# Cross-attention into a squared-ReLU layer on one core: w_out loaded by neighbouring rows, w_in read with a stride, the states loaded otherwise, and new lists

## The chip, the cores and the metric

The kernel runs on 1 core of one Trainium2 chip. The metric is the device time of one execution in microseconds (us). A core has five engines that run side by side, each through its own list of instructions: TensorE (PE; PEld is its weight load), VectorE (DVE), ScalarE (ACT), GpSimd (POOL) and SyncE (SP). Data moves by DMA; the profile calls GpSimd's queue a software queue, SyncE's and ScalarE's hardware queues. In this kernel the loads on GpSimd's queue turn float32 into float16 on the way, the others copy as it is.

## The reference, cut to what matters

For each of 8 batches there are 8 heads, 512 tokens `x` and 32 state slots, 64 values a head. Tokens read the states and states read the tokens, by a softmax each; what comes out (544 rows of 512 values a batch) goes through a two-layer network.

```python
scores = scale * np.matmul(x, state.transpose(0, 1, 3, 2))   # softmax over the 32 slots
xread = np.matmul(a, state)
...
scores2 = scale * np.matmul(state, x.transpose(0, 1, 3, 2))  # softmax over the 512 tokens
sread = np.matmul(a2, x)
...
h = x @ w_in                 # 4352 x 512 by 512 x 2048
r = np.maximum(h, 0.0)
g = s * (r * r) + b
return g @ w_out             # 4352 x 2048 by 2048 x 512
```

Here `x` of the network is `xread` and `sread` side by side over the heads. All inputs and the output are float32.

## The kernel before, in words

**The work.** The read of the tokens is never formed. For each batch b and each of the four chunks c of 512 columns of w_in, TensorE multiplies the states with w_in into `M` (`part_M`, line 718; `att_M`, 834): eight small matmuls, four column groups by two row groups of the array, side by side. Layer 1 (`layer1`, 961) then multiplies `M` with the normalised weights `a4` of the softmax (`att_scores`, 770), four groups of 128 features for a chunk; ScalarE applies ReLU (996), VectorE squares (1002). Layer 2 of batch 0 (`layer2_first`, 1178) is 64 plain matmuls of 512 columns, 16 for each quarter q of w_out. The other batches and the slots (`layer2`, 1235) use a scheme with seven products for eight, whose sums VectorE makes (`pair_sums`, 1073; `weight_sums`, 1108). `bias_sum` (1128) needs all of w_out. The slots' layer 1 comes last (`layer1_slots`, 1012), with w_in as the stationary operand: 64 matmuls of 256 columns.

**Features and rows.** Feature `128 f + p` of chunk c stands on partition p of block f of layer 1's output, so the matmuls of layer 2 need row `128 f + p` of quarter q of w_out on partition p, block f. `wo_load` (484) brings it so: each partition gets four rows that lie 128 rows apart, 2 KB of float32 each.

**Loads.** w_in comes in four chunks (`wi_load`, 472), w_out in four quarters (`wo_load`), each cast to float16 by GpSimd's queue, 512 KB where it lands. The first batch of `x` comes on SyncE's queue in four pieces (`x0_load`, 439) and is cast by ScalarE and VectorE. The states of batch 0 come on ScalarE's queue (409), those of batches 1 and 2 on GpSimd's (561), the others later on SyncE's (522). They are read as 64 values (256 bytes) at a time: each partition holds one slot of one of four heads.

**States' transposes** (`att_st`, 575). VectorE casts the states and writes them twice (602 on); TensorE transposes them through the identity into a float16 view of a PSUM pair (`is_transpose`); VectorE copies them to `stT`. Three sets: batch 0, batches 1 and 2, batches 3 to 7 (this one by DMA).

**Banks.** PSUM holds three pairs of banks (`pair`) and two single banks (`o`). `M` of most (b, c) goes to a pair and is copied out by one engine; those in `APART` (353) go to the two single banks and are copied by halves. Of batch 0, chunks 0 and 1 are copied by halves out of a pair (846).

**Order.** Nothing is scheduled by the compiler. Each piece of work is recorded as a numbered `op` with its cost, and `TURNS` (17) lists, engine by engine, in which order the numbers are issued. `Plan.order` (148) merges the five lists with those costs and with the planner's idea of when loads land, gives out buffers, and puts `fill` matmuls (403, with operands `warm`) into TensorE's list where it expects TensorE to wait in the first 20 us. An engine takes its instructions strictly in this order; a fill matmul is executed whether or not there is a wait. The loads at the start on GpSimd's list are, in order: w_in 0, states of batches 1 and 2, batch 1, w_in 1, w_out 0, w_in 2, w_out 1, w_in 3, w_out 2, w_out 3, batches 2 and 3. TensorE does M and layer 1 of chunk 0 of batch 0, batch 1's transposes between, then chunk 1, then batch 0's layer 2 mixed with layer 1 of chunks 2 and 3 and of batch 1.

Of the kernel before, what the change touches and what calls it, by code (L numbers as in the profile page):

```python
# [11 lines left out]
FP16 = mybir.dt.float16  # L12
# [6 lines left out]
        27 29 25 31 35 33 39 36 40 50 48 80-81 187 84-85 185 53 59 189 92-93 88-89 117 192 118 125-126 121  # L19
        113 122-123 127 119 68 70 114-115 124 116 128 193 120 96 141 129-130 99 237 131-133 225 74 134 142  # L20
        135 145 136 234 137 146 102 147 105 149 148 150-152 161-162 76 108 165-166 240 163 138 111 143
        167-168 164 243 139 222 144 72 62 157 140 158 153 159 56 228 154 160 231 173 155 174 1051 65 330 175
        156 169-171 267 333 258 334 259 268 260-263 269-270 172 176 271 264 272-274 348 351 1056 78 265 345
        354 360 286 277 287-289 694 445 278-281 290-291 282-284 339 357 292 342 293 295-299 454 567 1061
        305-306 300-301 307 302 308 696 576 452 309 315 310 316 311 317 312 318-322 570 572 1066 375-379 448
        689 450 384-387 380 476 388 381-382 467 479 464 389-390 394 482 395 461 391 470 396-397 403 398-401
        473 592 404-405 412 406-407 413-415 408-409 416 410 589 417-419 422 698 692 574 432-436 583 437
        423-424 438 425 439 426-428 586 429 604 601 506 497 507 711 595 498-499 508 598 509 500 510 501-504
        511-512 714 513 516-519 1071 1076 525-526 520-521 527 522-523 528 939 811 529-530 534 531-532
        535-541 544 820 932 935 554-556 545 557-561 546 720 723 619-621 726 622 547-549 705 550-551 623-626  # L30
        717 708 628-630 638-639 631-633 640 634-635 641-642 848 647 643 648-653 644-645 654 845 656-663 1086
        1081 937 941 666-668 676-677 669-670 814 816 818 671-672 678-680 673 954 681 836 741-744 682-683 830
        745-746 957 747 750 748 751-753 833 754-755 760 756 761-763 757 764-766 842 769-770 767 771-775
        778-781 776 782-785 839 788 798-799 789 800 790 801 827 969 963 791 802-805 951 960 1106 792 863 948
        864 793 865 794 866 795 867 1101 868-870 872-878 1091 882 879 883 966 884-888 891-892 1096 889
        893-898 900-906 910 907 911-915 920-921 916-917 1121 1111 984 922 1116 985-986 923 987 924-926
        988-989 927 990 1126 993 991 994-1000 1003-1010 1012-1019 1021-1028 1031-1035 1041 1036 1042
        1037-1038 1043-1048 1143-1150 1152-1159 1162-1169 1171-1178 1180-1187 1190-1197 1200-1207
    """,
    "ACT": """  # L40
        20-21 30 23 37 41 38 42 44 52 45 51 82 86 60 190-191 94 90 194-195 69 197-198 97 100 238 226 235 103
        106 77 109 241 244 223 63 57 229 232 67 331-332 335-336 349 352 79 346 361 355 695 447 446 340 358
# [4 lines left out]
    """,  # L47
    "DVE": """
        24 28 22 26 34 32 6 47 43 49 46 188 83 186 61 7 87 54-55 1057 91 71 95 196 199 98 75 1052 214 101
        239 210 104 215 206 236 107 207 227 110 252 112 218 209 179 177 64 73 245 58 219 242 224 1053 233 66  # L50
        220 230 246 216 253 325 337 183 208 181 247 1058 211 266 248 275 249 347 255 250 256-257 350 356 212
        217 213 285 221 1062 353 254 251 1067 294 341 457 1063 458 303 459 344 369 313 323 1068 363 370 364
        362 359 366 579 371 367 580 365 383 372 581 368 373 392 466 701 402 374 472 1072 484 463 478 469 411
        702 420 481 1077 485 703 475 491 440 585 430 494 594 488 495 492 489 486 588 487 606-608 713 505 597
        514 603 1078 496 493 616 524 940 490 533 1073 542 591 1082 610 936 562 823-824 600 825 944 552 613
        627 1087 617 722 611 945 614 719 636 609 946 728 716 646 615 612 655 707 618 1088 664 1083 942 725
        735 819 710 674 729 684 738 732-733 956 749 730 850 736 739 737 847 758 835 731 768 777 786 734 832
        838 854 740 841 860-861 844 971 959 806 829 855 857 1110 796 851 965 858 852 859 871 962 1105 880
        953 975 856 950 853 972 890 968 1108 899 1103 908 862 976-977 918 1100 981 1098 978 1118 973 1113
        982 928 983 992 979 1125 974 1001 1093 1120 980 1011 1128 1130 1095 1131 1020 1134 1123 1115 1135  # L60
        1029 1137 1140 1136 1138 1132 1141 1039 1049 1151 1160 1133 1142 1170 1139 1179 1188 1198 1208
    """,
    "POOL": """
        8-9 11 16 10 12-15 17-19 329 200 204 202 444 566 180 304 314 276 393 688 810 1060 421 441 182 431
        515 563 324 184 665 178 637 675 1065 1055 759 1070 1080 543 1075 1090 1085 807 685 909 881 919 553
        787 929 797
    """,
    "SP": """
        0-5 327 201 203 328 442 205 443 326 564 338 565 456 1059 687 686 578 460 1064 700 582 1054 704 930
        808-809 931 1079 822 943 1074 826 947 1084 1069 1089 1050 1040 1030 1161 1002 1189 1199 1209  # L70
# [16 lines left out]
class Plan:  # L87
# [60 lines left out]
    def order(self, fill):  # L148
# [3 lines left out]
        dma_free = {"sw": 7.05, "hw": 0.0}  # L152
# [5 lines left out]
        mode, out = "full", []  # L158
# [138 lines left out]
def kernel(  # L297
# [55 lines left out]
    APART = {(1, 0), (1, 1), (2, 0), (2, 1)}  # L353
# [40 lines left out]

    nc.vector.memset(warm, 0.0)
# [13 lines left out]
    nc.scalar.dma_start(stf[0], st_v[:, 0:NG, :])  # L409
    nc.scalar.preload_act_table_set("natural_log_exp_and_others")  # L410

    def T(u):
        return plan.tile(u)
# [7 lines left out]
    def copy(e, dst, src):  # L421
        (nc.scalar.copy if e == "ACT" else nc.vector.tensor_copy)(dst, src)  # L422


    MB, XB = 2.54, plan.XB
# [13 lines left out]
    def x0_load(i):  # L439
        op(  # L440
            {"SP": 0.5},
            lambda e: nc.sync.dma_start(xf_ap(i), x0_v[:, x0_heads(i)]),
            wr=[K(("xf", i))],
            dma=("hw", 0.75),
            lands=(3.6, 4.7, 6.0, 6.5)[i],
        )
# [25 lines left out]
    def wi_load(c):  # L472
        op(
            {"POOL": 0.85},
            lambda e: nc.gpsimd.dma_start(
                out=wi[c],
                in_=moe_w_in.rearrange("(k p) f -> p k f", p=P)[:, :, c * FC : c * FC + FC],
            ),
            rd=[g0],
            wr=[K(("wi", c))],  # L480
            dma=("sw", MB),
        )

    def wo_load(q):
        op(
            {"POOL": 0.75},
            lambda e: nc.gpsimd.dma_start(
                out=wo[q],
                in_=moe_w_out.rearrange("(q f p) n -> q p f n", p=P, q=4)[q],
            ),  # L490
            rd=[g0],
            wr=[K(("wo", q))],
            dma=("sw", MB),
        )
# [49 lines left out]
    for i in range(4):  # L544
# [14 lines left out]
    op(  # L559
        {"POOL": 0.9},  # L560
        lambda e: nc.gpsimd.dma_start(out=stf[1], in_=st_v[:, NG : NS * NG, :]),
        rd=[g0],
        wr=[K(("stf", 1))],
        dma=("sw", 0.45),
    )
# [9 lines left out]
    def att_st(i):  # L575
# [4 lines left out]
        def view():  # L580
            return T(u).rearrange("p a f -> p (a f)").bitcast(FP16).rearrange("p (n q) -> p n q", q=P)
# [4 lines left out]
        def tr(e):  # L586
            for k in range(n):
                mm(
                    view()[:, k, :],
                    st16[:, b0 * NG + k].rearrange("p k d -> p (k d)"),  # L590
                    ident16,
                    is_transpose=True,
                )
# [11 lines left out]
            since=(5.0, 0.0, 0.0)[i],  # L605
        )
        if i == 2:
# [14 lines left out]
            {"DVE": 0.1 + 0.07 * n},  # L622
            lambda e: copy(e, stT[:, b0 * NG : b1 * NG], view()[:, 0:n]),
# [210 lines left out]
    def att_M(b, c, engs=("ACT", "DVE")):  # L834
# [11 lines left out]
        if b == 0 and c < 2:  # L846
            for g in range(NG):
# [3 lines left out]
                    rd=[K(u)],  # L851
# [494 lines left out]
    att_scores(0)  # L1346
    att_st(1)
# [71 lines left out]
```

## Time and profile before

| | |
|---|---|
| median of 3 runs | 207.4 us (207.22 to 208.0) |
| the profiled execution: time | 208.01 us |
| its span, first to last instruction | 206.2 us |
| bytes moved | 25.83 MB, mean 125 GB/s |
| median issue to landing: w_in, w_out, `x` | 13.2, 17.4, 8.6 us |

The profile is of one execution. A row of its timeline has the start in us, the length, the engine, the line, the operation with output and inputs, the count, and in brackets how long the engine was idle before it and what ended that. Matmuls are pipelined: a row's length contains the way through the array, so the pace of a series is read from starts, not from lengths. All of TensorE's matmuls have line 335, that of a helper, and all plain copies line 422; they are told apart by the tiles' names.

### The profile page before, as it was taken

To read this page: it belongs to the slowest core of one execution; us is meant where nothing else is said; L and a number is where in the kernel's file an instruction comes from. 1 tells how busy PE (TensorE), PEld (TensorE's weight loads), DVE (VectorE), ACT (ScalarE), POOL (GpSimd) and SP (SyncE) were. 2 spreads that over 40 slices of the span, in tenths; PEclk is the share of its full clock that TensorE was granted. 3 is DMA by queue.
4 is the path that set the end of the run, shared out by engine and by line. 5 is a ranking of instruction groups with operands and counts; after the bars stand their busy time and mean duration, and the time that the engine had idled before them with its cause. 6 is when DMAs were issued, how large, how long until landed. Compare 5 with 4: busy or idle time off the path is not lost.

```text
span 206.2 us, 4768 instructions
## 1 busy us (share of the span) xinstructions
PE 199.3 (97%) x1989; PEld 134.7 (65%) x1989; DVE 164.3 (80%) x325; ACT 109.3 (53%) x153; POOL 38.8 (19%) x60
## 2 busy tenths in 40 slices
PE   7979999999999999999999999999999999999992
PEld 3744444435666665677577767766776688888881
DVE  2327637989899979899999988997969689859871
ACT  4757786467588879468644473254606634130000
POOL 4832002001020120331301030033070200331000
PEclk9999999999999999999999999999999999999999
DMA  5999999992999992798991470233020200253054
GB/s 173 201 197 204 206 205 179 179 198 16 186 139 195 143 221 41 110 134 154 199 194 60 80 222 13 51 111 118 0 103 3 102 0 2 71 187 105 0 176 131
DMA packets 47285, 25.83 MB, mean 125 GB/s; under 512 B 31616, under 2 KB 45440, under 8 KB 47264
## 3 DMA queue, kind: packets, MB, share of 16 engines
q0 software_dynamic: 13792, 15.34, 38.0%
q1 hardware_dynamic: 33056, 10.10, 26.4%
q8 instruction: 15, 0.25, 0.5%
q10 hardware_dynamic: 416, 0.10, 0.2%
q14 instruction: 6, 0.05, 0.1%
HBM read 17.33 MB, written 8.91 MB: 127 GB/s over the span
## 4 chain that ended last, share of the span: by engine, by line
PE 89%; DMA 7%; DVE 1%; issue 0%; ACT 0%; POOL 0%; DVEq 0%
PE o L335 48%; PE pair L335 41%; DMA wi<-in_moe_w_in_dram 4%; DMA out_dram<-osb 2%; DMA ident<-ident_const 1%; DVE osb L1281 0%; DVE M L422 0%; ACT M L422 0%; DVE osb L1270 0%; DVE aN L906 0%; DVE sr L933 0%; POOL gate L552 0%; DVEq L1270 0%
## 5 line engine op out<-in xcount | busy, mean ns | idle before, releaser
L996 ACT ACTIVATE g<-pair 128x1024 f16<-128x1024 f32 x64 | 63.0, 1023 | 44.5 <-PE pair L335 44.4
L335 PE MATMUL pair<-a,M 128*128 128x512 f16 x256 | 63.3, 379 | 0.1
L335 PEld LDWEIGHTS <-pd 128*128 128x128 f16 x480 | 46.4, 98 | 10.1 <-issue 1.5
L335 PEld LDWEIGHTS <-g 128*128 128x128 f16 x424 | 40.7, 98 | 17.5 <-issue 2.9
L1002 DVE TENSOR_TENSOR g<-g 128x1024 f16<-128x1024 f16 x64 | 42.8, 683 | 2.8 <-ACT g L996 2.8
L335 PE MATMUL o<-u,pd 128*128 128x256 f16 x360 | 44.2, 273 | 0.0
L335 PE MATMUL o<-wo,g 128*128 128x256 f16 (+1 forms) x272 | 42.6, 285 | 0.0
L335 PEld LDWEIGHTS <-M 128*128 128x128 f16 x256 | 24.7, 98 | 22.9 <-DVE M L422 0.6
L1173 POOL DMA_DIRECT2D out_dram<-osb x28 | 18.8, 724 | 103.2 <-DVE osb L1281 54.5
L1270 DVE SCALAR_TENSOR_TENSOR osb<-o,s,bias_bc 128x512 f32<-128x512 f32 (+1 forms) x32 | 22.9, 715 | 7.3 <-PE o L335 5.7
L422 ACT CAST M<-pair 128x1024 f16<-128x1024 f32 (+1 forms) x22 | 20.4, 958 | 7.8 <-PE pair L335 7.8
L1281 DVE SCALAR_TENSOR_TENSOR osb<-o,s,osb 128x512 f32<-128x512 f32 (+1 forms) x24 | 17.2, 716 | 7.6 <-PE o L335 7.4
L1082 DVE TENSOR_TENSOR pd<-g 128x1024 f16<-128x1024 f16 (+1 forms) x32 | 20.7, 651 | 0.1
L335 PE MATMUL o<-wo,pd 128*128 128x256 f16 x120 | 19.0, 273 | 0.0
L335 PE MATMUL o<-u,g 128*128 128x256 f16 x120 | 17.5, 273 | 0.0
L422 DVE CAST M<-pair 128x1024 f16<-128x1024 f32 (+1 forms) x8 | 9.2, 1153 | 4.9 <-PE pair L335 3.8
L1093 DVE TENSOR_TENSOR pd<-g,pd 128x512 f16<-128x512 f16 (+1 forms) x32 | 12.5, 400 | 0.1
L1043 ACT ACTIVATE g<-pair 128x256 f16<-128x256 f32 x16 | 5.3, 385 | 13.0 <-PE pair L335 13.0
L1090 DVE TENSOR_TENSOR pd<-g,pd 128x512 f16<-128x512 f16 (+1 forms) x32 | 12.1, 400 | 0.1
L782 ACT ACTIVATE E<-pair 128x512 f16<-128x512 f32 x16 | 9.5, 600 | 4.7 <-issue 2.3
L335 PE MATMUL pair<-wi,stT 64*32 64x512 f16 x224 | 9.8, 383 | 1.5 <-DMA wi<-in_moe_w_in_dram 1.2
L463 POOL DMA_DIRECT2D xn<-in_x_dram x7 | 6.3, 909 | 25.2 <-ACT g L996 15.1
(70 smaller groups left out, 143.7 us busy)
## 6 DMA issues: line engine op xcount, KB each, us to landing
out_dram<-osb POOLq DMA_DIRECT2D x28, 256.0 KB, 3.2
xn<-in_x_dram POOLq DMA_DIRECT2D x7, 512.0 KB, 8.6
wi<-in_moe_w_in_dram POOLq DMA_DIRECT2D x4, 512.0 KB, 13.2
wo<-in_moe_w_out_dram POOLq DMA_DIRECT2D x4, 512.0 KB, 17.4
u<-in_x_dram SPq DMA_DIRECT2D x4, 256.0 KB, 3.9
out_dram<-osb SPq DMA_DIRECT2D x4, 256.0 KB, 2.7
out_dram<-osb SPq DMA_DIRECT2D x4, 128.0 KB, 2.3
pd<-in_state_dram SPq DMA_DIRECT2D x1, 320.0 KB, 4.0
```

What stands on the lines that cost most here:

```text
L335: return nc.tensor.matmul(out, lhsT, rhs, start=start, stop=stop, tile_position=tp, is_transpose=is_transpose, skip_group_check=True,)
L422: (nc.scalar.copy if e == "ACT" else nc.vector.tensor_copy)(dst, src)
L463: lambda e: nc.gpsimd.dma_start(out=T(xn[b]).rearrange("p h c d -> p h (c d)"), in_=x[b].rearrange("h (q c) d -> q h (c d)", q=P),),
L782: nc.scalar.activation(T(E[b])[:, g, :].rearrange("p (m t) -> p m t", m=2), T(u)[:, :, hS * g : hS * g + hS], AF.Exp, scale=scale, accum_o ...
L996: lambda e, u=u, part=part: nc.scalar.activation(part(), T(u), AF.Relu),
L1002: lambda e, part=part: nc.vector.tensor_mul(part(), part(), part()),
L1082: nc.vector.tensor_tensor(view()[:, :, 0:2], blocks(b, j)[:, :, 1:2, :].to_broadcast((P, 2, 2, n)), blocks(b, j)[:, :, 0:4:3, :], ALU.subt ...
L1090: nc.vector.tensor_tensor(view()[:, :, 2], blocks(b, j)[:, :, 3], view()[:, :, 0], ALU.subtract)
L1093: nc.vector.tensor_tensor(view()[:, :, 3], blocks(b, j)[:, :, 2], view()[:, :, 2], ALU.subtract)
L1173: lambda e: eng(e).dma_start(dst, src()),
L1270: lambda e: nc.vector.scalar_tensor_tensor(t_view(u), o_view(bank), s_bc, bias(h), ALU.mult, ALU.add),
L1281: lambda e: nc.vector.scalar_tensor_tensor(t_view(u), o_view(bank), s_bc, t_view(u), ALU.mult, ALU.add),
```

## The change

w_out: a partition p now gets rows 4p to 4p + 3 of the quarter, 8 KB of float32 in one run. Feature `4p + f` of a chunk must then stand on partition p of block f, so `part_M` and `layer1_slots` read w_in's columns with a stride of four. The states of batches 0 to 2 are loaded as neighbouring rows too (two rows, 512 bytes, a partition for batch 0; four rows, 1 KB, for batches 1 and 2), and the transposes, now plain matmuls into float32, write every second or every fourth column so that the slots come out in the old order. The states of batches 1 and 2 leave GpSimd's queue; SyncE loads them after VectorE has written two elements of their buffer from batch 0's `E`. Chunks 1 to 3 of batch 0 join `APART`. The planner's costs change in places, and `TURNS` is new for all engines. Ops behind the states' load have new numbers.

GpSimd's order at the start is now w_in 0, 2, 3, 1, w_out 0, batch 1, w_out 1, w_out 2, w_out 3, batches 2 and 3. TensorE does M and layer 1 of all four chunks of batch 0 (chunks 0, 2, 3, 1), then w_out 0's matmuls, with the transposes of the states and of batch 1 among them, then w_out 1, batch 1's scores, w_out 2, w_out 3, and then layer 1 of batch 1. There are 57 fill matmuls in place of 59.

The diff without the lists and with the numbering lines left out:

```diff
@@ -149,7 +150,7 @@
         free = {"PE": 2.88, "ACT": 2.4, "DVE": 1.3, "POOL": 0.5, "SP": 0.6}
         queue = {e: self.turns(e)[::-1] for e in free}
         assert sum(map(len, queue.values())) == len(self.ops)
-        dma_free = {"sw": 7.05, "hw": 0.0}
+        dma_free = {"sw": 6.95, "hw": 0.0}
         big, flying, weights = 0.0, [], []
         landed = {"sw": [], "hw": []}
         slot_free = {t: [0.0] * len(s) for t, s in self.slots.items()}
@@ -350,7 +351,7 @@
     NM = 10
     NS = 3
     TURN = 3
-    APART = {(1, 0), (1, 1), (2, 0), (2, 1)}
+    APART = {(0, 1), (0, 2), (0, 3), (1, 0), (1, 1), (2, 0), (2, 1)}
     plan = Plan()
     plan.buffers("ps", ps)
     plan.buffers("o", ob)
@@ -392,6 +393,10 @@
     ident_dr = nc.inline_tensor(np.eye(P, dtype=np.float16), name="ident_const")
     st_v = state.rearrange("b (g hf) j d -> (hf j) (b g) d", g=NG)
 
+    def st_near(b0, b1):
+        rows = state[b0:b1].rearrange("b h j d -> (b h j) d")
+        return rows.rearrange("(q r) d -> q r d", q=P)
+
     nc.vector.memset(warm, 0.0)
     nc.vector.memset(few, 0.0)
     nc.vector.memset(ones16, 1.0)
@@ -406,7 +411,7 @@
     for _ in range(4):
         mm(ob[1], warm[:, 0:P], warm)
     nc.scalar.dma_start(ident16, ident_dr.ap())
-    nc.scalar.dma_start(stf[0], st_v[:, 0:NG, :])
+    nc.scalar.dma_start(stf[0], st_near(0, 1))
     nc.scalar.preload_act_table_set("natural_log_exp_and_others")
 
     def T(u):
@@ -422,7 +427,7 @@
         (nc.scalar.copy if e == "ACT" else nc.vector.tensor_copy)(dst, src)
 
 
-    MB, XB = 2.54, plan.XB
+    MB, WB, XB = 2.54, 1.95, plan.XB
 
     xf_u = [plan.unit(("u", i), "u") for i in range(2)]
     x0_v = x[0].rearrange("h (q c) d -> q h (c d)", q=P)
@@ -442,7 +447,7 @@
             lambda e: nc.sync.dma_start(xf_ap(i), x0_v[:, x0_heads(i)]),
             wr=[K(("xf", i))],
             dma=("hw", 0.75),
-            lands=(3.6, 4.7, 6.0, 6.5)[i],
+            lands=(3.75, 4.7, 5.95, 6.25)[i],
         )
 
     def x0_cast(i):
@@ -478,7 +483,7 @@
             ),
             rd=[g0],
             wr=[K(("wi", c))],
-            dma=("sw", MB),
+            dma=("sw", MB + 0.44 * (c == 3)),
         )
 
     def wo_load(q):
@@ -486,11 +491,11 @@
             {"POOL": 0.75},
             lambda e: nc.gpsimd.dma_start(
                 out=wo[q],
-                in_=moe_w_out.rearrange("(q f p) n -> q p f n", p=P, q=4)[q],
+                in_=moe_w_out.rearrange("(q p f) n -> q p f n", p=P, q=4)[q],
             ),
             rd=[g0],
             wr=[K(("wo", q))],
-            dma=("sw", MB),
+            dma=("sw", WB),
         )
 
     stf2 = plan.unit(("stf2",), "pd")
@@ -556,13 +561,6 @@
     g0 = K(("start",))
     wi_load(0)
     wi_load(1)
-    op(
-        {"POOL": 0.9},
-        lambda e: nc.gpsimd.dma_start(out=stf[1], in_=st_v[:, NG : NS * NG, :]),
-        rd=[g0],
-        wr=[K(("stf", 1))],
-        dma=("sw", 0.45),
-    )
     wo_load(0)
     wi_load(2)
     wo_load(1)
@@ -578,7 +576,7 @@
         n = (b1 - b0) * NG
 
         def view():
-            return T(u).rearrange("p a f -> p (a f)").bitcast(FP16).rearrange("p (n q) -> p n q", q=P)
+            return T(u)[:, 0, 0 : n * P]
 
         def src():
             return st_rows(n) if i == 2 else stf[i]
@@ -586,10 +584,9 @@
         def tr(e):
             for k in range(n):
                 mm(
-                    view()[:, k, :],
+                    view().rearrange("p (q r) -> p r q", r=n)[:, k],
                     st16[:, b0 * NG + k].rearrange("p k d -> p (k d)"),
                     ident16,
-                    is_transpose=True,
                 )
 
         key = K(("st", i))
@@ -602,7 +599,7 @@
             ),
             rd=[[], [K(("stf", 1))], [K(stf2)]][i],
             wr=[key],
-            since=(5.0, 0.0, 0.0)[i],
+            since=(4.1, 0.0, 0.0)[i],
         )
         if i == 2:
             part = slice(b0 * NG, b1 * NG)
@@ -619,8 +616,8 @@
         u = plan.unit(("stps", i), "ps")
         op({"PE": 0.056 * n}, tr, rd=[key], wr=[K(u)], mode="full", mms=n)
         op(
-            {"DVE": 0.1 + 0.07 * n},
-            lambda e: copy(e, stT[:, b0 * NG : b1 * NG], view()[:, 0:n]),
+            {"DVE": 0.07 + 0.135 * n},
+            lambda e: copy(e, stT[:, b0 * NG : b1 * NG].rearrange("p n q -> p (n q)"), view()),
             rd=[K(u)],
             wr=[K(("stT", i))],
         )
@@ -721,7 +718,7 @@
                 mm(
                     M_bank(b, c, g)[32 * q : 32 * q + 32],
                     st_T(b, g, q, g),
-                    wi[c][64 * g : 64 * g + 64, q],
+                    wi[c][64 * g : 64 * g + 64, q].rearrange("k (p f) -> k f p", f=4),
                     tp=(64 * g, 32 * q),
                 )
 
@@ -843,12 +840,12 @@
                     wr=[K(M[b, c], g)],
                 )
             return
-        if b == 0 and c < 2:
+        if b == 0:
             for g in range(NG):
                 op(
                     {"ACT": 0.48, "DVE": 0.64},
                     lambda e, g=g: copy(e, T(M[b, c])[:, g], T(u)[:, g]),
-                    rd=[K(u)],
+                    rd=[K(u)] + [K(M[b, c], 0)] * g,
                     wr=[K(M[b, c], g)],
                 )
             return
@@ -1020,7 +1017,7 @@
                     for k in range(NKM):
                         mm(
                             T(u)[:, 0, 256 * i : 256 * i + 256],
-                            wi[c][:, k, o : o + P],
+                            wi[c][:, k].rearrange("k (p f) -> k f p", f=4)[:, o // P],
                             srd[:, k].rearrange("p j b -> p (j b)"),
                             start=(k == 0 and i == 0),
                             stop=(k == NKM - 1),
@@ -1344,6 +1341,19 @@
     att_st(0)
     att_xT_pe(0)
     att_scores(0)
+    op(
+        {"DVE": 0.08},
+        lambda e: nc.vector.tensor_copy(stf[1][:, 0, 0:2], T(E[0])[:, 1, 0:2]),
+        rd=[K(E[0], 1)],
+        wr=[K(("stf", 1))],
+    )
+    op(
+        {"SP": 0.5},
+        lambda e: nc.sync.dma_start(out=stf[1], in_=st_near(1, NS)),
+        wr=[K(("stf", 1))],
+        dma=("hw", 0.4),
+        lands=16.6,
+    )
     att_st(1)
     for c in range(4):
         for b in range(3):
```

More of the change, by code (lines that the diff above doesn't have):

```diff
@@ L18 @@
     "PE": """
[L19 to L38, printed above, removed]
+        24 28 26 30 32 34-35 38 51 39 83 87 69 88 84 99 76 102 108 60 105 91-92 95-96 116-117 120 124 118
@@ new lines @@
+        121 125-126 49 119 127 190 128 188 122-123 129 136 132 137 192 72 138 130 133 139 134 131 196 195
+        152-155 135 148 140 149-150 144 79 111 168 151 164-165 246 169 166-167 114 145 141 170 240 171 237
+        142 54 146 243 63 225 143 147 228 156-157 57 74 160-162 234 231 163 176-177 158 333 66 1054 159
+        178-179 270-271 336-337 261 172 262 173 272-274 174 275 263-266 276 267 175 268 348 351 277 345 1059
+        342 289 354 280-281 290 282 291-292 448 81 699 283-284 293 285-286 294 287 295 357 298 457 697 296
@@ new lines @@
+        299-301 360 302 363 303-305 308 573 579 570 309 318 310-314 319 315 320 1064 451 453 321-325 378-379
+        692 455 575 380-383 387 470 388-389 464 479 390 384 391 467 473 385 392 695 1069 393 476 397-398 482
+        399-401 394 402 485 406-408 403 409-410 404 411 592 412-413 415-422 425 595 426 577 701 435 427
+        436-437 428 438-439 598 440 586 429 441-442 604 607 430 500-501 431-432 502-503 589 504-507 509-511
+        714 601 717 512-513 519 514-516 520-524 528 525-526 529-535 537 814 1074 1079 538-541 547 542-544
@@ new lines @@
+        942 935 938 548 557-558 549 559-564 711 550-551 723 552-553 622 729 554 720 726 631-632 623 633
+        624-625 634 626-629 823 944 819 635-637 641-642 638 708 643-646 650-652 647 653 648 654 848 655 851
+        656 659-660 657 661-666 669-670 1084 1089 821 940 817 679-682 671 683 836 684-685 672-676 830 686
+        839 753-754 744-745 755 746-748 960 749-751 833 756-759 763 760 764-765 842 766-767 772 768-769 773
+        770 774-775 845 776 781-782 777-779 783-788 791 957 801-804 954 792 805 793-794 969 795 806 796
@@ L39 @@
+        807-808 797 1104 798 1094 866-871 875 872-873 963 876-877 885 878-880 886 881 966 887 882 951 972
+        894 888-890 895-896 891 897-898 892 899-900 1099 903 901 904-910 913 1109 914 923-924 915 925-928
+        1119 916-917 929 918 930 1114 1129 919-920 987-990 1124 991 996-997 992-994 998-1003 1006-1013
+        1015-1022 1024-1030 1034 1031 1035-1041 1044-1051 1146-1153 1155-1162 1165-1172 1174-1181 1183-1190
+        1193-1200 1203-1210
     """,
     "ACT": """
-        20-21 30 23 37 41 38 42 44 52 45 51 82 86 60 190-191 94 90 194-195 69 197-198 97 100 238 226 235 103
@@ L42 @@
-        106 77 109 241 244 223 63 57 229 232 67 331-332 335-336 349 352 79 346 361 355 695 447 446 340 358
[4 rows of a table removed]
+        22 21 27 31 36-37 40-41 52 43-44 53 70 85 89 78 100 103 61 109 106 97 93 193-194 200 197-198 201 80
+        112 247 241 238 55 244 226 64 229 75 59 235 232 334-335 68 338-339 349 352 346 343 355 449-450 700
+        82 358 458 698 361 364 572 580 571 452 454 456 576 694 693 471 465 480 468 474 477 486 483 696 593
+        578 702 596 599 587 605 590 608 602 715 718 815-816 936-937 943 712 939 724 730 727 721 945 709 824
@@ L47 @@
+        820 852 849 941 818 822 831 840 834 837 843 846 961 958 955 1097 1107 1105 1095 970 964 952 1102 967
+        973 1110 1122 1112 1100 1120 1127 1130 1125 1132 1115 1117
     """,
     "DVE": """
-        24 28 22 26 34 32 6 47 43 49 46 188 83 186 61 7 87 54-55 1057 91 71 95 196 199 98 75 1052 214 101
-        239 210 104 215 206 236 107 207 227 110 252 112 218 209 179 177 64 73 245 58 219 242 224 1053 233 66
-        220 230 246 216 253 325 337 183 208 181 247 1058 211 266 248 275 249 347 255 250 256-257 350 356 212
@@ L52 @@
[L52 to L61, printed above, removed]
+        20 23 19 25 29 33 46 42 45 71 86 77 62 48 104 101 90 98 50 94 191 189 110 6 73 107 202 199 113 213
@@ new lines @@
+        221 7 1055 115 180 182 248 56 242 239 65 328 222 219 223 58 255 227 230 217 214 236 216 67 233 1060
+        209 245 186 249 1056 211 340 210 250 184 256 269 252-253 218 278 251 257 1061 220 258 224 215 259
+        1065 353 212 356 260 288 344 254 347 359 297 460-461 306 462 574 372 1066 316 350 369 373 326 370
+        365 362 582 366-367 583-584 466 1070 386 375-376 1071 368 472 475 469 395 704 405 488 414 478 1080
+        484 371 423 481 705 377 706 374 594 487 443 489-490 600 497 491 498 433 1075 494 492 591 597 495 508
@@ L62 @@
+        613 609 517 496 719 527 499 614 493 716 536 606 1081 1076 545 588 735 619 610 565 1085 603 826-827
[4 rows of a table added]
+        1103 995 1126 1101 986 1004 1133-1134 1014 1128 1116 1111 1121 1135 1023 1131 1136 1143 1118 983
+        1032 1144 1137-1138 1140 1139 1042 1052 1154 1141 1163 1173 1142 1145 1182 1191 1201 1211
     """,
     "POOL": """
-        8-9 11 16 10 12-15 17-19 329 200 204 202 444 566 180 304 314 276 393 688 810 1060 421 441 182 431
-        515 563 324 184 665 178 637 675 1065 1055 759 1070 1080 543 1075 1090 1085 807 685 909 881 919 553
@@ L66 @@
-        787 929 797
+        8-9 12 14 10-11 15 13 16-18 332 207 203 205 183 447 569 307 1068 317 279 1058 187 185 396 327 691
+        813 1063 434 444 566 640 181 668 424 1088 1078 688 556 546 1083 1073 1093 810 762 884 518 912 922
+        790 800 932 678
     """,
     "SP": """
-        0-5 327 201 203 328 442 205 443 326 564 338 565 456 1059 687 686 578 460 1064 700 582 1054 704 930
-        808-809 931 1079 822 943 1074 826 947 1084 1069 1089 1050 1040 1030 1161 1002 1189 1199 1209
+        0-5 47 208 204 331 330 206 329 446 1057 445 341 568 459 567 690 689 463 581 1067 1062 703 585 707
@@ L71 @@
+        811 933 812 934 825 1082 946 829 1077 1072 1087 950 1092 1005 1043 1053 1164 1033 1192 1202 1212
     """,
```

8 rows, old and new, of the table TURNS are left out of this document.

## The prediction

> **What bounds the kernel now.** I read the page first: the share of each engine and the chain that ended last.
>
> ```profile
> span 206.2 us, 4768 instructions
> PE 199.3 (97%) x1989; PEld 134.7 (65%) x1989; DVE 164.3 (80%) x325; ACT 109.3 (53%) x153; POOL 38.8 (19%) x60
> ...
> PEclk9999999999999999999999999999999999999999
> ...
> PE 89%; DMA 7%; DVE 1%; issue 0%; ACT 0%; POOL 0%; DVEq 0%
> PE o L335 48%; PE pair L335 41%; DMA wi<-in_moe_w_in_dram 4%; DMA out_dram<-osb 2%; DMA ident<-ident_const 1%; DVE osb L1281 0%; DVE M L422 0%; ACT M L422 0%; DVE osb L1270 0%; DVE aN L906 0%; DVE sr L933 0%; POOL gate L552 0%; DVEq L1270 0%
> ```
>
> TensorE is busy all the time at full clock, and the only transfer of weight on the chain is the first w_in chunk (4% of 206.2 is 8.3 us). So the change can earn time only where TensorE is busy with nothing. The table of busy time by stretches says where that is not:
>
> ```profile
> 20.00:48.00 28.00, 28.00 (x195) 11.47 (x197) 20.25 (x36) 19.48 (x23) 1.13 (x3) 1.00 1.14 183
> 48.00:90.00 42.00, 41.73 (x531) 27.05 (x532) 38.09 (x74) 32.60 (x47) 8.02 (x10) 1.00 0.87 134
> 90.00:140.00 50.00, 50.00 (x589) 35.33 (x588) 47.01 (x81) 26.69 (x34) 7.13 (x11) 1.00 0.60 127
> 140.00:202.20 62.20, 62.17 (x516) 50.30 (x514) 50.55 (x109) 18.49 (x30) 12.46 (x19) 1.00 0.22 72
> ```
>
> From 20 us on TensorE (first figure after the stretch) loses 0.3 us in 182. What is left is the opening. The timeline there, TensorE's own lines, shows real work and fill (`warm` operands):
>
> ```profile
> 11.72 0.41 PE L335 MATMUL pair<-wi,stT 64*32 64x512 f16 x8 [1.21 <-DMA wi<-in_moe_w_in_dram]
> ...
> 12.06 0.94 PE L335 MATMUL o<-warm 128*128 128x256 f16 x7
> ...
> 13.06 0.82 PE L335 MATMUL o<-warm 128*128 128x256 f16 x6
> ...
> 17.08 0.50 PE L335 MATMUL pair<-warm 128*128 128x256 f16 x3
> ...
> 18.07 0.72 PE L335 MATMUL pair<-warm 128*128 128x256 f16 x5
> ...
> 19.36 0.55 PEld L335 LDWEIGHTS <-M 128*128 128x128 f16 x4 [0.61 <-DVE M L422]
> ```
>
> The first chunk lands at 11.7 us; from there to 19.4 us there are 21 fill matmuls and short waits; from 19.4 us there is no gap. The question is how much real work stands done at the end of this opening, before and after.
>
> **The change part by part.** (1) *When data lands.* The tile view of the weights gives issue and time to landing.
>
> ```profile
> L475 POOL DMA_DIRECT2D wi<-in_moe_w_in_dram x4: 770/838/908, 3.4 to 9.0; - x4
> ...
> DMA to landing us min/median/max: 8.3/13.2/18.6
> ```
> ```profile
> L487 POOL DMA_DIRECT2D wo<-in_moe_w_out_dram x4: 760/768/861, 6.8 to 12.8; - x4
> ...
> DMA to landing us min/median/max: 13.2/17.4/19.8
> ```
> ```profile
> 14.88 0.45 PEld L335 LDWEIGHTS <-xn 128*128 128x128 f16 x8 [0.52 <-DMA xn<-in_x_dram]
> ```
>
> So w_in 0 lands at 3.4 + 8.3 = 11.7, w_out 0 at 6.8 + 13.2 = 20.0, w_out 3 at 12.8 + 19.8 = 32.6: five steps of 2.52 us. Batch 1 came 3.15 us behind w_in 0, with the states ahead of it. The changed GpSimd order is w_in 0, 2, 3, 1, w_out 0, batch 1, w_out 1, 2, 3. I keep w_in 0 at 11.7 (nothing ahead of it in its queue changes) and take the steps: w_in 2 at 14.2, 3 at 17.1 (0.4 for the states, which now cross from SyncE's queue; bounds 0 and 3.15 - 2.52 = 0.6), 1 at 19.7. What w_out costs with 8 KB runs no row shows; bounds 2.52 (today's) and 1.3 (half, for want of a row). I keep 2.5, since all loads of the trace run at one pace.
>
> (2) *The opening, walked.* Durations of ScalarE's steps, and the pace of TensorE:
>
> ```profile
> 9.17 0.59 ACT L782 ACTIVATE E<-pair 128x512 f16<-128x512 f32 x1
> ...
> 9.64 0.20 ACT L782 ACTIVATION_READ_ACCUMULATOR E<-pair 128x1 f32 x1
> ...
> 10.44 0.58 ACT L817 ACTIVATE o<-o 128x512 f32<-128x512 f32 x1
> ...
> 12.19 0.59 ACT L422 CAST M<-pair 128x512 f16<-128x512 f32 x1 [1.18 <-PE pair L335]
> ...
> 12.68 0.60 ACT L823 ACTIVATE a<-o 128x512 f16<-128x512 f32 x1
> ...
> 14.89 1.02 ACT L996 ACTIVATE g<-pair 128x1024 f16<-128x1024 f32 x1 [1.13 <-PE pair L335]
> ```
> ```profile
> 38.25 0.86 PE pair L335 x4
> ```
>
> A 512-wide matmul takes 0.86 / 4 = 0.216. In the new lists TensorE does M of chunk 0 at 11.7, the denominator's second half behind it, then layer 1 of chunks 0, 2 and 3 as they land. ScalarE has in a row from 12.2: M half, Ln, Exp, M half (14.6), M of chunk 2 (15.2), two ReLUs that wait for layer 1 (15.85 to 17.9), M of chunk 3 (18.5), two ReLUs (20.5), M of chunk 1 (21.1). TensorE reaches M of chunk 1 at 19.85, runs half of chunk 3's layer 1 to 21.1, waits 0.2 for that last M copy and 0.15 for a PSUM pair whose ReLU ends at 22.1, and ends layer 1 of batch 0 at 23.1. By then it has done 32 matmuls of layer 1 (6.9), four M groups (0.86) and a denominator (0.22): 8.0 us of work. Before, at 23.05 (row 22.83 below), it had done 16 of layer 1 (3.45), ten of layer 2 (2.16), batch 1's transposes (0.9), three M groups, scores, states' transpose and a denominator (1.3): 7.8 us. **Gain 0.1** (0.2 of work less 0.07 of time). Bounds: +0.8 if neither the states nor ScalarE hold it back (0.1 + 0.4 + 0.35), -0.6 if each of its three ReLU pairs meets a busy ScalarE by another 0.2.
>
> (3) *Behind the opening.* TensorE now meets w_out 0 at 23.1 (lands 22.2), batch 1 at 25.5 (24.9), w_out 1 at 27.3 (27.4), w_out 2 at 30.0 (29.9), w_out 3 at 32.5 (32.4). So faster w_out loads have cover already at today's pace: **worth 0** (bounds 0 and 0.2). Batch 1's scores now stand only some 1.8 us of matmuls ahead of the denominator that needs both their Exps (0.5 + 2 x 0.6 + 0.2 = 1.9): **loss 0.1** (0 to 0.4).
>
> (4) *Mode changes of the array* (whole to quarters and back). Two M groups in the trace:
>
> ```profile
> 22.83 0.38 PE L335 MATMUL o<-wo,g 128*128 128x512 f16 x1
> ...
> 23.14 0.63 PE L335 MATMUL pair<-wi,stT 64*32 64x512 f16 x16
> ...
> 23.70 0.60 PE L335 MATMUL o<-wo,g 128*128 128x512 f16 x2
> ```
>
> Entering costs 23.14 - (22.83 + 0.22) = 0.09, leaving 0.56 - 2 x 0.22 = 0.12. Counted over both lists, the number of changes behind the opening is the same (42). **0.**
>
> (5) *The stall that is left.*
>
> ```profile
> 75.81 0.41 PE L335 MATMUL pair<-wi,stT 64*32 64x512 f16 x8 [0.27 <-DVE sr L933]
> ```
>
> A bank is freed late by one VectorE step. The lists are new, so it goes or moves: **gain 0.1** (0 to 0.27).
>
> (6) *w_in read with a stride of four.* As the moving operand in all 32 M groups, as the weight in 64 loads of the last layer 1:
>
> ```profile
> L335 PEld LDWEIGHTS <-wi x64: 97/98/98, 161.5 to 184.9; 128*128 128x128 f16 x64
> L335 PE MATMUL pair<-srd,wi x64: 272/273/273, 161.7 to 185.0; 128*128 128x256 f16 x64
> ```
>
> No strided read of either kind is in the trace. Below: 0, as nothing can be read faster than packed. Above: twice, 32 x 0.22 = 7.0 us for the M groups, and 64 x (0.196 - 0.109) = 5.6 us for the loads, which would then outlast their matmuls (0.109, half of 0.216). I take **0**, the packed row. [...]
>
> (7) *States' transposes* now write every second or fourth fp32 column of PSUM instead of packed fp16.
>
> ```profile
> 5.95 0.28 PE L335 MATMUL pair<-ident,st 128*128 128x128 f16 x2
> ...
> 12.84 0.39 PE L335 MATMUL pair<-ident,st 128*128 128x128 f16 x4
> ...
> 13.26 0.42 DVE L422 COPY stT<-pair 128x512 f16<-128x512 f16 x1 [0.41 <-PE pair L335]
> ```
>
> Only the four of batches 1 and 2 are in gapless time, at some 0.06 each: **0**, at most 0.2 if the writes double. [...] The copy behind them reads fp32 and costs up to 0.69 instead of 0.42 on VectorE, with over 1 us until the scores need it.
>
> (8) One GpSimd load of states (0.76) goes; a SyncE load and a tiny VectorE copy come. SyncE's next work is a transpose of batch 1's scores, much later: 0.
>
> Sum: -0.1 + 0.1 - 0.1 = **-0.1**. The profiled execution took 208.01 us around its span of 206.2; the three runs shown have a median of 207.4. From the median: **207.3 us**.
>
> **The rivals.** *Faster:* ScalarE and the states never hold TensorE back, and the stall at 75.8 goes: 0.8 + 0.27, so 206.3. For it: copies of M now have banks of their own on both engines. Against: the walk finds ScalarE without a gap from 18 to 21 us. *Slower, w_in's stride:* one mechanism, TensorE's reads at 8-byte steps. It decides once eight M matmuls take over 0.25 us (32 x 0.03 = 1 us); at twice it is 207.3 + 7.0 + 5.6 = 219.9. For it: nothing in the trace is read like this. Against: four fp16 apart is close. *Slower, the lists slip:* the opening's bound of 0.6, the scores' 0.4, PSUM's 0.2 and no gain at 75.8: 208.7. For it: ScalarE's order is rigid, and SyncE's states cross the weights. *w_out no faster than now:* the change doesn't do what it may look like; by (3) still 207.3 to 207.5.
>
> **How the numbers follow.** Forecast 0.43, w_out no faster 0.05, faster 0.27, lists slip 0.15, stride 0.10. 0.5% (1.04 us) is about what a measurement of this kernel tells from no change. Faster 0.27, within 0.48, slower 0.25. The range goes from the faster rival, less the 0.2 by which a run lies under the median, to the slipped lists: 206.1 to 208.7; it leaves out the stride and little else. The forecast's own range is 206.7 to 207.9.
>
> **What would show it.** M groups of eight at 0.22 apart and weight loads of `wi` at 98 ns (6); w_in 1 landing near 19.7 (1); the first `wo` matmul near 23 with about 17 or more fill matmuls behind 11.7 (2); no TensorE wait on a `wo` load (3); TensorE gapless from there to 202. Wrong would be: w_in 0 landing a microsecond earlier or later than 11.7, a gap over 0.3 us behind 25 us, or M groups that stretch.

## The result, and the profile after

The changed kernel takes 215.13 us (median of 4 runs, 214.62 to 215.87) against 207.31 us beside it: 1.0382 times as long, with a 95% interval of 1.0329 to 1.0435. It is slower by 7.8 us, far outside the range on record.

The page of the changed kernel, the span, the engines' shares, the clock and the chain:

```profile
span 213.7 us, 4755 instructions
...
PE 206.8 (97%) x1987; PEld 135.6 (63%) x1987; DVE 161.1 (75%) x322; ACT 113.5 (53%) x159; POOL 36.8 (17%) x59
...
PEclk9999999999999999999999999999999999999999
...
PE 94%; DMA 3%; SPq 1%; DVE 1%; issue 0%; ACT 0%
```

TensorE is as full as before (97%), at full clock, and is now 94% of the chain. Its busy time grew by 206.8 - 199.3 = 7.5 us, the span by 7.5 us. TensorE's idle time is 6.9 us in both profiles (206.2 - 199.3 and 213.7 - 206.8), so it isn't waiting that was added: the work takes longer. The tile view of w_in says which work. Before:

```profile
L335 PE MATMUL pair<-wi,stT x224: 372/386/388, 11.7 to 137.7; 64*32 64x512 f16 x112
```

After:

```profile
L336 PE MATMUL pair<-wi,stT x200: 605/621/665, 11.7 to 143.9; 64*32 64x512 f16 x100
L336 PEld LDWEIGHTS <-wi x64: 112/113/117, 168.1 to 191.8; 128*128 128x128 f16 x64
L336 PE MATMUL pair<-srd,wi x64: 272/273/273, 168.2 to 191.9; 128*128 128x256 f16 x64
L336 PE MATMUL o<-wi,stT x56: 605/606/608, 14.4 to 50.1; 64*32 64x512 f16 x56
```

The matmuls of the M groups, which stream w_in with the stride, went from a median of 386 ns to 606 and more. The 64 weight loads went from 98 to 113 ns, and the matmuls that they feed stayed at 273. TensorE's own lines of the opening, in the changed kernel:

```profile
8.99 0.62 PE L336 MATMUL pair<-ident,xn 128*128 128x128 f16 x8 [1.10 <-ACT xn L427]
...
11.75 0.63 PE L336 MATMUL pair<-wi,stT 64*32 64x512 f16 x8
12.31 0.39 PE L336 MATMUL o<-E,bones 128*128 128x512 f16 x1
12.54 0.82 PE L336 MATMUL pair<-warm 128*128 128x256 f16 x6
...
14.37 0.63 PE L336 MATMUL o<-wi,stT 64*32 64x512 f16 x8
14.93 1.90 PE L336 MATMUL pair<-a,M 128*128 128x512 f16 x8
16.67 0.82 PE L336 MATMUL o<-warm 128*128 128x256 f16 x6
17.41 0.63 PE L336 MATMUL o<-wi,stT 64*32 64x512 f16 x8
...
20.15 0.63 PE L336 MATMUL o<-wi,stT 64*32 64x512 f16 x8
...
23.32 0.81 PE L336 MATMUL o<-wo,g 128*128 128x512 f16 x3
```

A group of eight holds the array 12.31 - 11.75 = 0.56 us; before it was 12.06 - 11.72 = 0.34. That is 0.22 more, the time of a whole stream of 512 columns, and 32 groups make 7.0 us, which lies within the 6.8 to 9.0 us that the interval of the ratio allows. The first matmul with w_out starts at 23.3, close to the 23.1 of the walk, but by chance; the account of step (2) below says why.

### The profile page after: what moved, and what is told of

Read it like the earlier page. It is cut to its first block, busy times and chain, and to the rows that moved or that the text cites. A ratio compares the mean times of both kernels' runs of the same rounds, so it can differ in the third digit from the quotient of the medians.

```text
span 213.7 us, 4755 instructions
## 1 busy us (share of the span) xinstructions
PE 206.8 (97%) x1987; PEld 135.6 (63%) x1987; DVE 161.1 (75%) x322; ACT 113.5 (53%) x159; POOL 36.8 (17%) x59
## 4 chain that ended last, share of the span: by engine, by line
PE 94%; DMA 3%; SPq 1%; DVE 1%; issue 0%; ACT 0%
PE o L336 50%; PE pair L336 43%; DMA u<-in_x_dram 3%; SPq L447 1%; DVE osb L1210 0%; ACT xn L427 0%; DVE osb L1267 0%
## 5 line engine op out<-in xcount | busy, mean ns | idle before, releaser
L993 ACT ACTIVATE g<-pair 128x1024 f16<-128x1024 f32 x64 | 63.7, 1026 | 36.1 <-PE pair L336 35.7
L336 PE MATMUL o<-wo,g 128*128 128x256 f16 (+1 forms) x272 | 41.2, 285 | 0.0
L1170 POOL DMA_DIRECT2D out_dram<-osb x28 | 19.3, 760 | 107.0 <-DVE osb L1278 67.2
L427 ACT CAST M<-pair 128x1024 f16<-128x1024 f32 (+1 forms) x24 | 22.6, 980 | 10.0 <-PE pair L336 9.9
L336 PE MATMUL pair<-wi,stT 64*32 64x512 f16 x200 | 14.2, 619 | 0.0
L1087 DVE TENSOR_TENSOR pd<-g,pd 128x512 f16<-128x512 f16 (+1 forms) x32 | 12.8, 403 | 0.1
L1090 DVE TENSOR_TENSOR pd<-g,pd 128x512 f16<-128x512 f16 (+1 forms) x32 | 12.7, 405 | 0.0
L336 PE MATMUL pair<-wo,g 128*128 128x512 f16 x32 | 10.4, 380 | 0.6 <-DVE osb L1210 0.6
L336 PE MATMUL o<-warm 128*128 128x256 f16 (+1 forms) x55 | 9.7, 327 | 1.2 <-DVE few L401 1.2
```

The lines of the kernel that those rows point to most:

```text
L336: return nc.tensor.matmul(out, lhsT, rhs, start=start, stop=stop, tile_position=tp, is_transpose=is_transpose, skip_group_check=True,)
L993: lambda e, u=u, part=part: nc.scalar.activation(part(), T(u), AF.Relu),
L1087: nc.vector.tensor_tensor(view()[:, :, 2], blocks(b, j)[:, :, 3], view()[:, :, 0], ALU.subtract)
L1090: nc.vector.tensor_tensor(view()[:, :, 3], blocks(b, j)[:, :, 2], view()[:, :, 2], ALU.subtract)
L1170: lambda e: eng(e).dma_start(dst, src()),
```

## The experiments

Two theories stood at the start. **A**: TensorE takes a strided moving operand in at half speed; that alone is the loss. **B**: the new lists, the new order of loads or the states' loads cost the time. A third, **C**, blamed the strided weight loads. Runs with several executions have a ratio to the kernel before, with its interval; the others ran once.

**The stride alone, in the old kernel.**

```diff
-                    wi[c][64 * g : 64 * g + 64, q],
+                    wi[c][64 * g : 64 * g + 64, q].rearrange("k (p f) -> k f p", f=4),
```

> The kernel before with one edit: the M groups read w_in with a stride of four as the moving operand; features come out permuted against w_out, so the output is not the reference's. Theory A (a strided moving operand is taken in at half speed): each of the 32 groups of eight matmuls takes 0.22 us longer, 207.3 + 7.1 = 214.4 us, and a matmul of such a group shows 0.6 instead of 0.38 us. Rival B (the new lists and the new order of loads cost the time): 207.3. Rival C (the strided weight loads of the slots' layer 1 cost it): 207.3.

Measured: 214.35 us, ratio 1.0324 (1.0279 to 1.0369), that is 6.7 us by the ratio. The same tile view of this kernel:

```profile
L335 PE MATMUL pair<-wi,stT x224: 605/607/628, 10.3 to 142.7; 64*32 64x512 f16 x112
L335 PEld LDWEIGHTS <-wi x64: 97/98/98, 166.7 to 190.1; 128*128 128x128 f16 x64
```

Old lists, old loads, packed weight loads, and the M matmuls at 607 ns: nearly all of the loss (5.8 to 7.7 of the 7.8 us) is there without anything else of the change. B and C cannot explain it.

**The change without the stride.**

```diff
-                    wi[c][64 * g : 64 * g + 64, q].rearrange("k (p f) -> k f p", f=4),
+                    wi[c][64 * g : 64 * g + 64, q],
...
-                            wi[c][:, k].rearrange("k (p f) -> k f p", f=4)[:, o // P],
+                            wi[c][:, k, o : o + P],
...
-                in_=moe_w_out.rearrange("(q p f) n -> q p f n", p=P, q=4)[q],
+                in_=moe_w_out.rearrange("(q f p) n -> q p f n", p=P, q=4)[q],
```

> The changed kernel with w_out loaded as before and w_in read packed again; lists, order of loads and the states' loads stay. Theory A: 215.1 - 7.1 = 208.0 us. Rival B: about 215. What is left above or below 207.3 is the price of lists, loads and states together: my forecast's own sum said -0.1.

Measured: 208.11 us, ratio 1.001 (0.9982 to 1.0038). Lists, order of loads and states together are worth nothing that can be measured. Theory B is out from this side too. TensorE comes to w_out earlier here (21.9 us, not 23.3) and waits for it once:

```profile
26.68 0.59 PE L336 MATMUL o<-wo,g 128*128 128x512 f16 x2 [0.30 <-DMA wo<-in_moe_w_out_dram]
```

**The change with the stride moved to where weights are loaded.** Feature `4p + f` is picked when layer 1 loads M, and w_in streams packed:

```diff
-                    wi[c][64 * g : 64 * g + 64, q].rearrange("k (p f) -> k f p", f=4),
+                    wi[c][64 * g : 64 * g + 64, q],
...
-                                T(M[b, j])[:, g, P * f : P * f + P],
+                                T(M[b, j])[:, g].rearrange("k (p f) -> k f p", f=4)[:, f],
```

> The changed kernel with w_out by neighbouring rows, but w_in read packed as the moving operand; the stride of four is taken where layer 1 loads M as weights (256 loads) and stays in the slots' weight loads. Theory A (only the moving operand pays): a strided weight load took 113 ns and layer 1 has 216 ns a matmul to hide it, so 208.0 us. Rival A2 (any strided operand pays in full): the loads of M would show about 200 ns and still hide below 216: also 208, but PEld rows tell. Rival B: 215.

Measured: 208.31 us, ratio 1.0012 (0.9987 to 1.0038). The tile view of M, first in the kernel before, then in this one:

```profile
L335 PEld LDWEIGHTS <-M x256: 95/98/99, 13.8 to 170.4; 128*128 128x128 f16 x128
L335 PE MATMUL pair<-a,M x256: 379/379/390, 13.8 to 170.7; 128*128 128x512 f16 x128
```
```profile
L336 PEld LDWEIGHTS <-M x256: 110/113/133, 12.0 to 169.5; 128*128 128x128 f16 x128
L336 PE MATMUL pair<-a,M x256: 378/379/408, 12.0 to 169.7; 128*128 128x512 f16 x128
```

256 strided weight loads at 113 ns in place of 98 pass beside matmuls whose 379 ns are those of before, where they start 216 ns apart. The same stride cost 6.7 us on one operand and nothing that can be measured on the other.

**Strided weight loads in the slots alone.**

```diff
-                            wi[c][:, k, o : o + P],
+                            wi[c][:, k].rearrange("k (p f) -> k f p", f=4)[:, o // P],
```

> The kernel before with one edit: the 64 weight loads of the slots' layer 1 read w_in with a stride of four (those rows of the output are not the reference's). Theory A: loads of 113 instead of 98 ns beside matmuls at 109 ns each, at most 64 x 0.004 = 0.3 us: 207.3 to 207.6. Rival C (weights pay double): 207.3 + 5.6 = 212.9.

Measured: 208.35 us, ratio 1.0021 (0.9983 to 1.0058). Theory C's 5.6 us are excluded; whether there is a cost of 0.3 us this cannot tell.

**The new layout in the old lists**, with the stride in the weight loads of both places (edits as above, and `wo_load` by neighbouring rows):

> The kernel before, its lists and states' loads untouched, with w_out by neighbouring rows, w_in packed as the moving operand and the stride of four only in weight loads (M in layer 1, w_in in the slots). Theory A: no dearer than the kernel before but for the slots' 0.3: 207.3 to 207.6; w_out landing no earlier than 32.6, since the changed kernel's w_out steps are 2.3 to 2.6 us. Rival (8 KB runs do help this order): down to 207.0.

Measured: 207.54 us, ratio 0.9993 (0.9967 to 1.0018): the same. The layout by neighbouring rows costs and brings nothing that can be measured (-0.7 to +0.4 us). One part of the expectation missed: w_out 3 had landed by 31.5, not 32.6, since the loads began earlier; from 19.0, where w_out 0 landed, five steps to there are 2.5 us each, as before. This was the only version that might have beaten both kernels; it doesn't by anything that can be measured.

**Other strides, and the whole array.** The edit is that of the first experiment with `f=2`, `f=8` and `f=16`.

> The kernel before with w_in read at a stride of two (4 bytes) in the M groups; output not the reference's. Theory A1 (any step other than one is taken at half speed): 0.6 us a matmul, 214.4 us. Theory A2 (the price grows with the bytes passed over; steps up to 4 bytes are free): 207.3. Middle: 1.5 times the stream of 0.213, +3.4, 210.7.

Measured: 207.69 us, ratio 1.0002 (0.9978 to 1.0026).

> As before it, with a stride of eight (16 bytes). Theory A1 (half speed for any step): as stride four, 0.6 us a matmul, about 214.4 us. Theory A2 (price by bytes passed over): the stream doubles again to 0.85, a matmul shows about 1.0 us, 207.3 + 32 x 0.64 = 228.

Measured: 229.02 us. Theory A as first worded, half speed for any step, is wrong both ways: with a step of two a matmul of the M groups takes 395 ns where packed takes 386, and with a step of eight it takes 1056, a stream of (1056 - 386 + 216) / 216 = 4.1 times the packed one. Then layer 1's moving operand, on the whole array:

```diff
-                                T(a4[b])[:, g],
+                                T(a4[b])[:, g].rearrange("k (p f) -> k f p", f=4),
```

> The kernel before with layer 1's moving operand (the weights a4, 512 columns, whole array, one stream at a time) read with a stride of four; tokens come out permuted, so the output is not the reference's. Theory A general (each strided stream runs at half speed): 256 matmuls at 0.43 instead of 0.216: 207.3 + 55 = 262 us. Rival A tiled (it costs only where eight small matmuls read side by side): 207.3.

Measured: 267.63 us, 59.9 above the 207.8 beside it, 0.234 us for each of 256 matmuls, a little more than the 0.216 that was expected. So it isn't the eight small matmuls side by side; one stream alone on the whole array pays as well. This left the question of what is counted, the bytes passed over or the pieces fetched:

> The kernel before with w_in read at a stride of sixteen (32 bytes) in the M groups; output not the reference's. So far the rows of the M matmuls are 383 (packed), 395 (stride 2), 606 (4) and 1055 ns (8), times 207.8, 207.7, 214.4 and 229.0 us. Theory L (TensorE's operand comes in pieces of 16 bytes, each piece taking the time of four columns; a stride of eight already needs a piece for each column): no worse than stride eight, 1055 ns and 229. Theory B (the price follows the bytes passed over): the stream doubles once more to 1.71, a matmul shows 1.9 us, 207.8 + 32 x 1.5 = 256.

Measured: 229.49 us. From a step of 16 bytes to one of 32 the price hardly grew (1073 ns a matmul where stride eight had 1056). That is theory L's number; the theory B of this expectation, a price by the bytes passed over, asked for 256.

> The kernel before with layer 1's moving operand a4 read at a stride of two, whole array; tokens come out permuted, so the output is not the reference's. Theory L (four columns from one piece of 16 bytes are enough): 207.8, matmuls at 379 ns. Rival (only the eight small matmuls of an M group take stride two for nothing): between 220 and 235.

Measured: 209.93 us against 208.04. Near theory L but not nothing; the matmuls in the tile view of M are at 387 ns where they were at 379, and 256 x 0.008 = 2.0 us:

```profile
L335 PE MATMUL pair<-a,M x256: 386/387/399, 12.6 to 172.6; 128*128 128x512 f16 x128
```

The last two keep neighbours together, with `"k (p f r) -> k f p r"`, `f=4` and `r=4` or `r=2`:

> The kernel before with the M groups reading w_in as runs of four neighbouring columns (8 bytes), a run every 32 bytes; output not the reference's. Theory L (pieces of 16 bytes, 1.7 ns each, against 0.42 ns a column: four columns from one piece keep pace): 383 to 395 ns a matmul, 207.8 to 208.3 us. Rival (the step of 32 bytes counts, not the columns a piece gives): 600 to 1070 ns, 214 to 229 us.

Measured: 208.66 us (207.55 beside it). That is 0.4 above the expected range, from one execution of each; executions of the kernel before lay between 206.5 and 209.4.

> As before it, with runs of two neighbouring columns (4 bytes), a run every 16 bytes. Theory L (two columns from a piece, as at a stride of four): 606 ns, 214.4 us. Rival (the step of 16 bytes counts, as at a stride of eight): 1055 ns, 229 us. Second rival (neighbours within a run are enough): 383 to 395 ns, 207.8 us.

Measured: 213.78 us. In these runs neither the step nor having a neighbour sets the price; it goes with how many columns that follow one another in the stream lie in the same 16 bytes. The M matmuls of all these kernels, from the tile view of w_in in each: stride two, eight and sixteen, then runs of four and of two.

```profile
L335 PE MATMUL pair<-wi,stT x224: 382/395/401, 11.5 to 137.9; 64*32 64x512 f16 x112
```
```profile
L335 PE MATMUL pair<-wi,stT x224: 1052/1056/1077, 11.7 to 158.0; 64*32 64x512 f16 x112
```
```profile
L335 PE MATMUL pair<-wi,stT x224: 1071/1073/1097, 11.5 to 158.5; 64*32 64x512 f16 x112
```
```profile
L335 PE MATMUL pair<-wi,stT x224: 387/399/405, 11.3 to 138.4; 64*32 64x512 f16 x112
```
```profile
L335 PE MATMUL pair<-wi,stT x224: 605/607/628, 10.8 to 143.3; 64*32 64x512 f16 x112
```

Four columns from 16 bytes (stride two, runs of four) took 395 to 399 ns, two (stride four, runs of two) 607, one (stride eight or sixteen) 1056 to 1073. Step 16 bytes with pairs cost the same 607 as step 8 bytes without.

## Why the prediction was wrong, step by step

**Step (6) failed.** It took 0 for the strided read of w_in, "the packed row", between 0 and 7.0 us for the M groups, and gave its rival a chance of 0.10. The runs put the price at the upper end: 0.22 us a group, 7.0 us by the groups' length, 6.7 us by the run that has nothing else. The range left this end out, though the step itself had no row that spoke for 0. Taking the packed row as nearest was the error: no row of the old trace reads with a step, so nothing in it decided between the two ends, and an operand that sets TensorE's pace on a chain that is 89% TensorE deserved the larger share of the chances.

Its lower bound held: no strided row of the runs lies below its packed one; they lie 8 to 687 ns above. For the moving operand of the M groups, two float16 from 16 bytes ran at 607 ns a matmul and four at 395 to 399; packed, it is 386.

The upper end's second part, 5.6 us for the slots' weight loads, did not come: 113 ns a load, not 196, and no change in the matmuls' 273. The rival had the place and the mechanism, and one of its two prices.

**Step (1)** held in its paces and missed its start. GpSimd's rows of the changed kernel, and between them the landing times from the tile view of w_out:

```profile
2.94 3.17 POOL L480 DMA_DIRECT2D wi<-in_moe_w_in_dram  x4
6.09 0.55 POOL L492 DMA_DIRECT2D wo<-in_moe_w_out_dram  x1
...
10.59 0.54 POOL L492 DMA_DIRECT2D wo<-in_moe_w_out_dram  x1 [1.97 <-DMA wi<-in_moe_w_in_dram]
```
```profile
DMA to landing us min/median/max: 14.7/19.3/20.4
```
```profile
30.89 0.34 POOL L507 COPY aT<-wo 128x2 f16<-128x2 f16 x1 [14.36 <-DMA wo<-in_moe_w_out_dram]
```

w_out 0 landed at 6.1 + 14.7 = 20.8 and w_out 3 at 30.9: four loads (batch 1, w_out 1, 2, 3) in 10.1 us, 2.5 each, the pace of before. Runs of 8 KB were no faster here than runs of 2 KB (2.52 a step before), as the step took it. But w_in 0 landed by 10.6, where a wait of GpSimd for a w_in load ends, not at 11.7. That, the M groups that stretched and the stall under step (5) are the three signs of being wrong that the prediction had named; all three came. In the old lists with the new layout the loads also began earlier than in the profiled run of before (2.65 us against 3.41); that start moves from run to run, and why is open.

**Step (2)** met its end, 23.1, by luck. The kernel with the stride in the weight loads has the same lists, loads and layout, and packed M groups:

```profile
10.80 0.41 PE L336 MATMUL pair<-wi,stT 64*32 64x512 f16 x8
...
21.59 0.81 PE L336 MATMUL o<-wo,g 128*128 128x512 f16 x3
```

With w_in packed the lists need 10.8 us from the first M group to w_out, not the walk's 11.4, and begin 0.9 before it. In the changed kernel the same stretch takes 23.32 - 11.75 = 11.57, about 0.8 more for its four strided M groups. Its first group started late for another reason: TensorE waited at 8.99 for ScalarE's cast of the second half of `x`, not for w_in 0, which had landed by 10.6. The step's small gain isn't visible in the time: with w_in packed as the moving operand, the rest of the change, layout included, lies between -0.3 and +0.8 us (1.0012, 0.9987 to 1.0038), which holds the forecast's -0.1.

**Step (3)** held, with less cover than it counted: in the changed kernel TensorE never waits for w_out, and the new layout in the old lists gave 0.9993; but with w_in packed the lists reach w_out 1.2 to 1.5 us before the walk, and one of the two such kernels shows the wait of 0.30 above. The 0.1 that the step took off for batch 1's scores isn't seen: TensorE waits for no denominator. **Step (5)** was half wrong: the stall at 75.8 went, and another, 0.36 longer, came, in the timeline of the changed kernel:

```profile
53.97 0.38 PE L336 MATMUL pair<-wo,g 128*128 128x512 f16 x1 [0.63 <-DVE osb L1210]
```

**Step (7)**: the four transposes of the later states hold TensorE 25.44 - 25.04 = 0.40 us where they held it 13.06 - 12.84 = 0.22:

```profile
25.04 0.60 PE L336 MATMUL pair<-ident,st 128*128 128x128 f16 x4
...
25.44 0.42 PE L336 MATMUL o<-wo,g 128*128 128x512 f16 x1
```

That is the step's upper bound of 0.2, not its 0. These transposes now write every fourth column of PSUM, and they also became plain matmuls into float32; no run here tells the two apart. In the total it is too small to measure.

Nothing in the traces speaks against the 0 of **steps (4) and (8)**, and no run prices them alone. The sum for the slipped lists, 207.4 + 0.6 + 0.4 + 0.2, is 208.6 and not 208.7, which changes nothing.

## What to carry to other kernels

When a layout is changed to please a load, ask which operand pays for the new order. In this kernel TensorE's moving operand came near the packed 386 ns with four float16 of each 16 bytes (395 to 399) and not with two (607), while a stride of four in weight loads that hide behind their matmuls (113 ns a load for 98) cost nothing that could be measured (ratios 1.0012 and 1.0021). An operation that the trace doesn't show, on the engine that is the bound, is priced at the full range and given chances to match; one edit that tries it alone would have settled this at the start. And look whether the load gets faster at all: here w_out took 2.5 us a quarter in runs of 2 KB and of 8 KB alike.

## What the runs showed of the hardware

In these runs the price of a strided moving operand follows one number. Take the pace of 0.216 us for 512 packed columns, add what each kernel's matmul row gained on its packed one, and divide by the number of 16-byte pieces that hold its columns, a piece counted again each time the stream comes back to it. For stride four on the whole array the pace is read from starts, (101.26 - 99.47) / 4 = 0.448:

```profile
99.47 1.97 PE L335 MATMUL pair<-a,M 128*128 128x512 f16 x4
101.26 0.84 PE L335 MATMUL o<-wo,g 128*128 128x256 f16 x6
```

| columns of w_in or a4 | gain, us | pieces | ns a piece |
|---|---|---|---|
| stride two (whole array, 387 for 379) | 0.008 | 128 | 1.75 |
| stride two (M groups, 395 for 386) | 0.009 | 128 | 1.76 |
| runs of four (399 for 386) | 0.013 | 128 | 1.79 |
| stride four, runs of two (607 for 386) | 0.221 | 256 | 1.71 |
| stride four (whole array, by starts) | 0.232 | 256 | 1.75 |
| stride eight (1056 for 386) | 0.670 | 512 | 1.73 |
| stride sixteen (1073 for 386) | 0.687 | 512 | 1.76 |

About 1.75 ns a piece in all seven, so four packed columns' worth (4 x 0.216 us / 512 = 1.7 ns). The rows of stride four on the whole array, a median of 632 ns for 379, would give 1.83; why they are longer than the starts say is open. That the operand is fetched in such pieces is a picture that fits every run here, not something that a trace shows; other types and an alignment off 16 bytes were not tried. Weight loads of 128 columns at a stride of four took 113 ns for 98.
